# Loads and copies in pieces behind the value blocks of an attention kernel, its heads turned a block later

## The chip, the cores and the metric

One core of a Trainium2 chip runs the kernel. Its time is the device time of one execution in microseconds. TensorE (PE) multiplies matrices, VectorE (DVE), ScalarE (ACT) and GpSimd (POOL) do the rest, and SyncE (SP) issues every DMA, in one queue, in order. 16 DMA engines move the bytes.

## The reference

A token matrix of 2048 x 512 is layer-normalised. One branch is softmax attention with 32 heads of 16, the other a bilinear feed-forward of width 1792; the output is `x + attention * silu(feed-forward)`.

```python
xn = layernorm(x)
q, k, v = heads(xn @ wqkv)                    # 32 heads of 16
s = (softmax(q @ k.T * 16 ** -0.5) @ v) @ wo
g = silu(((xn @ w_gate) * (xn @ w_up)) @ w_down)
out = x + s * g
```

All is float32. Matmuls that need the precision run on rounded values (F32R) and their rests: `a = hi + lo`, three products in place of one.

## The kernel before, in words

**Units and tiles.** Attention goes by 32 units: a group of four heads (8 groups, `g`) times a quarter of the queries (`c`). Unit `i` is group `i // 4`, quarter `i % 4`. Each unit has 16 key tiles of 128; counted through, there are 512 tiles, `n`. For each tile and head one score matmul `t` (line 751) gives 128 keys x 512 queries, ScalarE takes its exponential into `e` (line 753), and `pv` (line 772; `last` in the last unit) multiplies `e` by the values. The maximum that the exponential needs is folded into the matmul as two more rows of `qs`. For that, all scores are computed a first time the other way round (`s`, line 729), 86 matmuls ahead of the `t`, and VectorE reduces each (`mx`, line 731). When a unit's maxima are complete, `maxima(i)` reduces and transposes them (`mm`, `mt`), stores them (`MD<-mt`) and loads them back as rows (`qs<-MD`).

**Cycles.** The main loop takes five tiles a cycle: 20 `t`, 20 `s` and a *filler*, a pair of sums with 24 to 30 matmuls in each half of the array's rows. Their order within a cycle is written out in `ORDERS`, or dealt evenly by `even` where the table has no entry. A cycle ends with `values`: the value matmuls of its five tiles, with other engines' steps placed before and behind them (`before_values`, `behind_values`). The filler, a generator, gives first the remaining projections (`p`, `proj_pair`), then the feed-forward (`g`, `u`, `y`), then the output product of the quarters that are done (`z`, `ending`). `Filler.begin` says at a cycle's start how many of the pair's matmuls the cycle takes. Where the generator yields nothing, because what the next pair needs isn't ready, the cycle has no filler.

**Order.** TensorE, ScalarE, VectorE and GpSimd run in program order. SP isn't in the list of ordered engines: up to tile 17 its DMAs are tied to program order (`Tied.on = n < 18`), later a scheduler orders them, and a DMA can be issued far ahead of its place in the program, once its buffers and data allow.

**What the change touches.**

- `proj_pair` copies two projections out of PSUM (`qr`); behind the value block `store` splits each into `hl` (one buffer) and `qk_store` writes it to DRAM (`KD<-hl`, `QD<-hl`).
- `load_k(g)` reads a group's keys from `KD` into one of two buffers `ks`. For groups 0 and 1 that is done by quarters of the keys, from group 2 on in two DMAs of 768 KB. It stands at the first tile of a group's second unit, for the group after. Scores of the next group begin 21 tiles ahead of it.
- The rounded inputs of quarters 1 to 3, `xh` and `xl`, are copied to DRAM (`XD`), six DMAs of 1 MB, each pair behind one of the projections of cycles 2 to 4, not before that projection's copy (`BEHIND`). The feed-forward reads them back later.
- `finish(i)` turns a unit's summed values: transpose `tr` (line 799), reciprocal, product on GpSimd, transpose back (line 810), store `OD<-acc`. It is a generator that `values` advances, once before and once behind the block. When it ends, the unit is `finished`, and `prepare` may load its heads for the output product.
- In the last cycles: 501 to 505 has the pair `z2_0`, 506 to 509 has `z2_2`, 510 and 511 have none.

Of the kernel before, what the change touches and what calls it, by code (L numbers as in the profile page):

```python
# [31 lines left out]
LEAD = 86  # L32
PAIRS = 4 * (NG // 2 - 1) + 1 + NC * (NF + 6)
BLOCK = 5
SOON = 8
ORDERS = {
# [30 lines left out]
}  # L67
SHORT = {65: 3, 68: 3}
HALF = (65, 491)
EBUFS = 20  # L70
HBUFS = 1
QBUFS = 2
# [12 lines left out]
def body(ctx, tc, x, wqkv, wo, wg, wu, wd, out):  # L85
# [512 lines left out]
    def ending():  # L598

        fp = fst["fp"]  # L600
        hi, lo = [fp.tile([P, 5, 512], F32R, name=n) for n in ("hl", "dh")]
        kept, added = [fp.tile([P, 5, 512], F32, name=n) for n in ("hh", "dl")]
        ops[0] = [(hi[:, d], lo[:, d]) for d in range(ND)]
        wrh, wrl = hi[:, 4], lo[:, 4]
        side = keep.tile([P, 2, 4, 512], F32, name="ks0")
        turn = [0]

        def until(c):
            while len([v for v in split_done if v[0] == c]) < ND:
                yield  # L610

        def rows_of(c, t):
            return x[(4 * c + t) * P:(4 * c + t + 2) * P].rearrange("(t p) d -> p t d", p=P)

        def two_tiles(c, t):
            yield from until(c)
            here = side[:, turn[0] % 2]
            turn[0] += 1
            got = [(here[:, n], here[:, 2 + n]) for n in range(2)]

            def loads():
                dma(here[:, 0:2], YD[c][:, t:t + 2])
                dma(here[:, 2:4], rows_of(c, t))
            soon(2, loads)
            two = Pair([("misc", f"z{c}_{u}") for u in (t, t + 1)], [o_terms(c, u) for u in (t, t + 1)])
            yield two
            for n, o in enumerate(two.outs):
                before_values.append(lambda u=t + n, o=o, got=got[n]: end(c, u, o, *got))

        rest = {}  # L630

        def begin_pair(t):
            yield from until(NC - 1)
            sums, more = [[tile[:, t + n] for n in range(2)] for tile in (kept, added)]
            rest.update({t + n: (sums[n], more[n]) for n in range(2)})
            for n in range(2):
                tt = 4 * (NC - 1) + t + n
                soon(2, lambda n=n, tt=tt: dma(more[n], x[tt * P:(tt + 1) * P]))
            ts = [o_terms(NC - 1, u) for u in (t, t + 1)]
            two = Pair([("misc", f"z{NC - 1}_{u}") for u in (t, t + 1)], [a[:-3] for a in ts], [a[-3:] for a in ts])  # L640
            yield two
            outs = two.outs
            nc.scalar.activation(sums[0], outs[0], AF.Copy)
            before_values.append(lambda: nc.vector.tensor_copy(sums[1], outs[1]))

        def gate_pair(t):
            for u in (t, t + 1):
                sums, more = rest[u]
                pool.tensor_tensor(sums, sums, fst["y"][:, u], op=OP.mult)
                pool.tensor_tensor(sums, sums, more, op=OP.add)  # L650

        yield from begin_pair(0)
        yield from begin_pair(2)
        ops[1] = small_tiles()
        wr = fp.tile([P, D], F32, name="wdr", bufs=2)
        pool.memset(wr, 0.0)
        for j in range(4):
            dma(wr[32 * j:32 * j + DH], wo[(H - 4 + j) * DH:(H - 3 + j) * DH])
        yield from two_tiles(0, 0)
        yield from two_tiles(0, 2)  # L660
        ops[2] = ops[0]
        behind_values.append(lambda: gate_pair(0))
        yield from two_tiles(1, 0)
        behind_values.append(lambda: gate_pair(2))

        def last_rows():
            pool.tensor_copy(wrh, wr)
            pool.tensor_tensor(wrl, wr, wrh, op=OP.subtract)
            for j in range(0, P, 32):
                dmar(wrh[j + DH:j + 32], wrh[j:j + DH])  # L670
        behind_values.append(last_rows)
        yield from two_tiles(1, 2)
        yield from two_tiles(2, 0)
        yield from two_tiles(2, 2)
        while "t" not in fst:
            yield
        banks = []
        for t in range(4):
            banks.append(psum("b", f"z{NC - 1}_{t}"))
            for n, r in enumerate((wrh, wrl)):  # L680
                nc.tensor.matmul(banks[t], fst["t"][:, t * P:(t + 1) * P], r, start=n == 0, stop=n == 1)
        Tied.on, sync.last, pool.last = True, None, None
        for t in range(4):
            end(NC - 1, t, banks[t], fst["y"][:, t], rest[t][0])
# [16 lines left out]
    def load_k(g, cs=range(NC)):  # L701
        heads = slice(64 * (g % 2), 64 * (g % 2) + 64)
        for e in range(2):
            k = ks[g % 2][64 * e:64 * e + KB]
            if g < 2:
                for c in cs:
                    dmar(k[:, :, c * 512:(c + 1) * 512], two(KD[0][c][heads], e))
            else:
                dmar(k, two(KD[g // 2][heads], e))

    def other_keys(_):
        ks.append(keep.tile([P, 2, S], F32R, name="ks1"))
# [48 lines left out]
    def part_block(i, todo):  # L761

        g = i // NC
        whole = i == NU - 1
        if whole and todo[0][1] == 0:
            fst["last"] = psum("s", "last")
        o = fst["last"] if whole else psum("b", f"pv{i}")
        for n, (_, kt, es) in enumerate(todo):
            halves = [slice(0, 256), slice(256, 512)] if whole and kt == NT - 1 else [slice(0, 512)]
# [20 lines left out]
    def finish(i):  # L790

        g, c = divmod(i, NC)
        tr = keep.tile([P, 16, 32], F32, name="tr", bufs=1)
        acc = sums.pop(i)
        late = i >= NU - NC
        flat = "p b e -> p (b e)"
        if not late:
            yield
        nc.vector.transpose(tr.rearrange(flat), acc)
        rc = keep.tile([P, 16, 1], F32, name="rc", bufs=1)  # L800
        if NU - NC <= i < NU - 2:
            yield
        nc.vector.reciprocal(rc, tr[:, :, DH:DH + 1])  # L803
        over = rc.to_broadcast([P, 16, DH])
        (nc.vector if i >= NU - NC else pool).tensor_tensor(tr[:, :, 0:DH], tr[:, :, 0:DH], over, op=OP.mult)
        if not late:
            yield
        elif i < NU - 2:
            yield
        nc.vector.transpose(acc, tr.rearrange(flat))  # L810
        dma(OD[c][4 * g:4 * g + 4], acc)
        finished.add(i)
# [150 lines left out]
    def filler(wq0):  # L963
        yield from proj_pair(0, [(wq0, 0, 2), (wq0, 0, 3)])
        for m in range(1, NG // 2):
            wk, wq = fst["qk", m]
            for c in range(NC):
                if c == 2 and m + 1 < NG // 2:
                    fst["qk", m + 1] = qk_weights(m + 1, 1), qk_weights(m + 1, 0)
                yield from proj_pair(m, [(wk, 1, c), (wq, 0, c)])  # L970
                if m == 1 and c:
                    after = fst["high"].ins.name
                    for n, src in enumerate((xh, xl)):
                        put = sync.dma_start(XD[c][n].bitcast(F32), src[c].bitcast(F32))
                        tc.add_manual_dep(put.ins, after, BEHIND, reason="not before the first exponentials")
                if m == NG // 2 - 1 and c == NC - 2:
                    nxt = gu_weights(0)
        run_all(before_values)
        run_all(behind_values)
        flush()  # L980
        qkv.close()
        fst["fp"] = ffp.enter_context(tc.tile_pool(name="ffn", bufs=1, reuse_waits="tile"))
        yield from ffn(nxt)

    finished = set()
    now = [0]
    heads, last_group = [], []

# [4 lines left out]
    class Filler:  # L993
# [6 lines left out]
            if self.pair is self:  # L1000
                self.pair, self.done = None, True

        def begin(self, whole):

            if not self.pair and not self.done:
                self.fetch()
            if not self.pair:
                return [0, 0]
            left = self.pair.left()
            return left if whole or left[0] <= self.pair.first[0] else list(self.pair.first)  # L1010

        def item(self, h):
            self.pair.emit(h)
# [3 lines left out]

    def values(rounds):
        run_all(before_values)
        step_small(heads)  # L1020
        run_all(reduced)
        if gates:
            gates.pop(0)()
        block(rounds)
        run_all(behind_values)
        step_small(heads)

    ready, reduced, gates = {}, [], []

# [3 lines left out]
    def place(h):  # L1033
# [6 lines left out]
        if n not in ready:  # L1040
# [2 lines left out]
            if kt == 6 and i + 2 < NU:  # L1043
                load_q(i + 2)
            if kt == 0 and g + 1 < NG and c == 1:
                load_k(g + 1)
            ready[n] = i, kt, [None] * 4
        es = ready[n][2]
        es[j] = expo(i, kt, j)
# [31 lines left out]
    with tc.manual_schedule(engines=ORDERED):  # L1081
# [4 lines left out]
        while n < NU * NT:  # L1086
            tiles = min(SHORT.get(n, BLOCK), NU * NT - 2 - n) or 2
            ends = n + tiles == NU * NT
            if m == TOTAL and place_of:
                place_of.close()  # L1090
                place_of = ctx.enter_context(banks_of(LATE_BUFS)) and None
            if fil.done:
                fil = Filler(ending())
            f = fil.begin(n not in HALF)
            last = min(4 * (n + tiles), TOTAL - 4 * (not ends))
            nt, ns = last - q, min(last + LEAD, TOTAL) - m
            q, m = q + nt, m + ns
# [21 lines left out]
        while fil.pair or not fil.done:  # L1119
# [2 lines left out]
            if not fil.pair:  # L1122
                fil.fetch()
            while fil.pair:
                for h, left in enumerate(fil.pair.left()):
                    if left:
                        fil.item(h)
                        break
            flush()
    ffp.close()  # L1130

# [15 lines left out]
```

## Time and profile before

| | |
|---|---|
| median of 3 runs | 1699.65 us (1699.35 to 1699.77) |
| the profiled execution | 1698.56 us |
| its span | 1696.8 us |
| TensorE busy, mean granted clock | 98% of the span, 0.992 |
| VectorE, ScalarE, GpSimd busy | 84%, 70%, 43% |
| DMA | 145.93 MB, 86 GB/s over the span |
| key loads | 16 of 192 KB, 12 of 768 KB |
| stores of `hl` | 30 of 512 KB and 30 of 256 KB |

The profile was taken in one execution, whose time stands 1.1 us under the median. TensorE's busy time says that it was at work, not that it ran at its peak. Rows of a chain give start, duration, engine, line; rows of waits give total, times, longest; rows of SP give start and the time that issuing took, and say nothing of when the bytes landed.

### The profile page before, as it was taken

What the parts mean: (1) busy time and instruction counts of PE and PEld (TensorE: products, weight loads), DVE (VectorE), ACT (ScalarE), POOL (GpSimd) and SP (SyncE); (2) the same over time, 40 slices, a digit from 0 to 9 for tenths busy, and PEclk for the clock granted to TensorE, in tenths of its full rate; (3) what the DMA queues carried; (4) which work ended last, traced back from release to release, by engine and by line L of the source; (5) the groups of instructions that cost most, each with busy time, mean ns of one, the idle gap of its engine ahead of it and who ended that gap; (6) DMA issues with size and microseconds to landing.
All of it is one profiled execution on the core that took longest, in us unless ns stands there. A gap on an engine that the chain in (4) does not pass through costs nothing.

```text
span 1696.8 us, 35187 instructions
## 1 busy us (share of the span) xinstructions
PE 1664.9 (98%) x13702; PEld 1125.1 (66%) x13702; DVE 1422.0 (84%) x2477; ACT 1189.3 (70%) x2553; POOL 736.6 (43%) x772
## 2 busy tenths in 40 slices
PE   9999899799999999999999999999999999999997
PEld 6776577466766666667666766676667666766654
DVE  7888698688888998889889888898889888888942
ACT  6367577576776777677677876776778676777775
POOL 5213343552542637346252653534347254446361
PEclk9999899899999999999999999999999999999999
DMA  6217533521222322412025221331325121133231
GB/s 232 89 48 210 214 135 113 146 73 30 66 68 58 95 70 80 79 54 62 23 71 128 80 61 36 81 58 52 104 61 118 30 66 46 47 99 104 71 116 69
DMA packets 117843, 145.93 MB, mean 86 GB/s; under 512 B 12781, under 2 KB 74477, under 8 KB 114989
## 3 DMA queue, kind: packets, MB, share of 16 engines
q1 hardware_dynamic: 117676, 143.69, 29.3%
q8 instruction: 108, 1.77, 0.4%
q14 instruction: 59, 0.48, 0.1%
HBM read 95.94 MB, written 47.45 MB: 85 GB/s over the span
## 4 chain that ended last, share of the span: by engine, by line
PE 89%; DVE 5%; DMA 2%; issue 1%; POOL 1%; ACT 0%; SPq 0%; DVEq 0%; POOLq 0%; ACTq 0%
PE pv L772 24%; PE s L729 15%; PE t L751 13%; PE u L354 10%; PE g L354 9%; PE y L354 8%; DVE mx L731 4%; PE p L354 4%; PE z L354 2%; DMA KD<-hl 1%; PE last L772 1%; PE v L306 1%; PE v L326 1%; PE v L330 1%; PE p L306 1%
## 5 line engine op out<-in xcount | busy, mean ns | idle before, releaser
L731 DVE TENSOR_REDUCE mx<-s 128x1 f32<-128x512 f32 x2048 | 1245.1, 684 | 170.4 <-PE t L751 127.6
L753 ACT ACTIVATE e<-t 128x512 f32<-128x512 f32 x2048 | 1025.4, 659 | 34.0 <-PE t L751 27.8
L751 PE MATMUL t<-qs,ks 50*128 50x512 f32 x2048 | 789.5, 406 | 3.3 <-DVE mx L731 0.9
L729 PE MATMUL s<-ks,qs 48*128 48x512 f32 x2048 | 757.8, 407 | 9.2 <-ACT part L785 5.3
L729 PEld LDWEIGHTS s<-ks,qs 48*128 48x128 f32 x2048 | 369.5, 186 | 145.4 <-issue 79.0
L772 PE MATMUL pv<-e,V 128*32 128x512 f32 x3968 | 446.5, 595 | 0.0
L751 PEld LDWEIGHTS t<-qs,ks 50*128 50x128 f32 x2048 | 374.8, 186 | 68.9 <-ACT e L753 16.5
L99 POOL TENSOR_TENSOR acc<-acc,part 128x512 f32<-128x512 f32 x93 | 120.5, 1295 | 445.4 <-ACT part L785 445.4
L772 PEld LDWEIGHTS pv<-e,V 128*32 128x32 f32 x3968 | 118.7, 110 | 265.0 <-issue 256.0
L785 ACT ACTIVATE part<-pv 128x512 f32<-128x512 f32 x93 | 55.7, 598 | 327.4 <-PE pv L772 314.9
L354 PE MATMUL g<-fh,w1h 64*128 64x512 f32 x448 | 180.9, 404 | 0.0
L354 PE MATMUL u<-fh,w0h 64*128 64x512 f32 x448 | 177.3, 396 | 0.0
L354 PE MATMUL g<-fh,w1l 64*128 64x512 f32 x448 | 177.1, 395 | 0.0
L354 PE MATMUL g<-fl,w1h 64*128 64x512 f32 x448 | 177.0, 395 | 0.0
L354 PE MATMUL u<-fl,w0h 64*128 64x512 f32 x448 | 176.5, 394 | 0.0
L354 PE MATMUL u<-fh,w0l 64*128 64x512 f32 x448 | 175.5, 392 | 0.0
L354 PE MATMUL y<-dh,hl 64*128 64x512 f32 x448 | 146.9, 393 | 0.0
L354 PE MATMUL y<-dh,hh 64*128 64x512 f32 x448 | 144.6, 395 | 0.0
L354 PE MATMUL y<-dl,hh 64*128 64x512 f32 x448 | 143.6, 394 | 0.0
L99 POOL TENSOR_TENSOR tr<-tr,rc 128x256 f32<-128x256 f32 x28 | 17.4, 622 | 220.6 <-DVE rc L803 220.6
L354 PEld LDWEIGHTS g<-fh,w1l 64*128 64x128 f32 x448 | 83.8, 187 | 5.5
L354 PEld LDWEIGHTS g<-fh,w1h 64*128 64x128 f32 x448 | 83.3, 186 | 4.3
(228 smaller groups left out, 2341.6 us busy)
## 6 DMA issues: line engine op xcount, KB each, us to landing
w1r<-in_wg_dram SPq DMA_DIRECT2D x56, 256.0 KB
w0r<-in_wu_dram SPq DMA_DIRECT2D x56, 256.0 KB
wdr<-in_wd_dram SPq DMA_DIRECT2D x56, 256.0 KB
qs<-QD SPq DMA_DIRECT2D x64, 192.0 KB
ks<-KD SPq DMA_DIRECT2D x12, 768.0 KB
KD<-hl SPq DMA_DIRECT2D x16, 512.0 KB
OD<-acc SPq DMA_DIRECT2D x31, 256.0 KB
QD<-hl SPq DMA_DIRECT2D x14, 512.0 KB
```

What stands on the lines that cost most here:

```text
L99: got = getattr(self.engine, name)(*args, **kw)
L306: nc.tensor.matmul(o[:, part], l(d), r(d)[:, part], start=k == d == 0 and not begun, stop=k == 2 and d == ND - 1, skip_group_check=begun)
L326: nc.tensor.matmul(outs[k], l[LOWER], r[LOWER], start=k == 0 and n == 0, stop=(stop or k == 0) and n == len(low) - 1, skip_group_check=k == 1)
L330: nc.tensor.matmul(outs[1 - k], l[UPPER], r[UPPER], start=k == 0 and m == 0, stop=(stop or k == 0) and m == len(high) - 1, skip_group_chec ...
L354: nc.tensor.matmul(self.outs[k], l[rows], r[rows], start=opens and not half, stop=closes, skip_group_check=half == 1)
L729: nc.tensor.matmul(o, QS[i][b:b + KB, pr, t * P:(t + 1) * P], k[b:b + KB, pr, kc * 512:(kc + 1) * 512], start=True, stop=True)
L731: nc.vector.tensor_reduce(MX[i][:, j, t, kc:kc + 1], o, axis=AX.X, op=OP.max)
L751: nc.tensor.matmul(o, k[b:b + KR, pr, kt * P:(kt + 1) * P], QS[i][b:b + KR, pr], start=True, stop=True)
L753: nc.scalar.activation(e, o, AF.Exp, scale=DH ** -0.5)
L772: nc.tensor.matmul(o[32 * j:32 * j + 32, c], V[:, kt, h0:h0 + 32], es[j][:, c], start=(kt if whole else n) == 0, stop=kt == NT - 1 if whol ...
L785: nc.scalar.activation(part, o, AF.Copy)
```

## The change

Key loads from group 2 on are cut into quarters like those before; all go through a list, `bulk`, at whose front they are put, and of which `values` runs up to four entries behind a block. The copies of the inputs are cut into pieces of 256 KB, go through the same list, and lose their dependency on the projection's copy. `values` advances the heads once, not twice, runs complete maxima ahead of them, and `finish` loses its first pause. `SOON`, from 8 to 12, lets maxima run in the middle of a cycle that ends up to two tiles ahead of a unit. The table `LIMIT` takes the place of `HALF`; the bank `last` is taken earlier; the last loop takes the longer half first and runs the waiting steps.

```diff
-SOON = 8
+SOON = 12
...
-HALF = (65, 491)
+LIMIT = {65: 12, 491: 12}
+BULK = 4
...
         yield from two_tiles(2, 2)
+        yield
         while "t" not in fst:
...
-                dmar(k, two(KD[g // 2][heads], e))
+                for c in cs:
+                    part = slice(c * 512, (c + 1) * 512)
+                    dmar(k[:, :, part], two(KD[g // 2][heads][:, :, part], e))
...
-        if whole and todo[0][1] == 0:
-            fst["last"] = psum("s", "last")
...
         flat = "p b e -> p (b e)"
-        if not late:
-            yield
         nc.vector.transpose(tr.rearrange(flat), acc)
...
-                    after = fst["high"].ins.name
-                    for n, src in enumerate((xh, xl)):
-                        put = sync.dma_start(XD[c][n].bitcast(F32), src[c].bitcast(F32))
-                        tc.add_manual_dep(put.ins, after, BEHIND, reason="not before the first exponentials")
+                    bulk.extend(lambda n=n, src=src[c], c=c, d=d: dma(XD[c][n][:, d].bitcast(F32), src[:, d].bitcast(F32))
+                                for n, src in enumerate((xh, xl)) for d in range(ND))
...
         run_all(behind_values)
+        run_all(bulk)
         flush()
...
-            if not self.pair:
-                return [0, 0]
-            left = self.pair.left()
-            return left if whole or left[0] <= self.pair.first[0] else list(self.pair.first)
+            return [min(limit, n) for n in self.pair.left()] if self.pair else [0, 0]
...
         run_all(before_values)
+        run_all(reduced)
         step_small(heads)
-        run_all(reduced)
         if gates:
             gates.pop(0)()
         block(rounds)
         run_all(behind_values)
-        step_small(heads)
+        for _ in range(BULK):
+            if bulk:
+                bulk.pop(0)()
...
-                load_k(g + 1)
+                bulk[:0] = [lambda g=g, c=c: load_k(g + 1, [c]) for c in range(NC)]
...
+                fst["last"] = psum("s", "last")
...
-                for h, left in enumerate(fil.pair.left()):
-                    if left:
-                        fil.item(h)
-                        break
+                left = fil.pair.left()
+                fil.item(left.index(max(left)))
+            run_all(before_values)
+            run_all(behind_values)
             flush()
```

More of the change, by code (lines that the diff above doesn't have):

```diff
@@ L983, in filler @@
         yield from ffn(nxt)
-    finished = set()
+    bulk, finished = [], set()
     now = [0]
@@ L1001, in fetch, with begin @@
                 self.pair, self.done = None, True
-        def begin(self, whole):
+        def begin(self, limit):
             if not self.pair and not self.done:
                 self.fetch()
-            if not self.pair:
-                return [0, 0]
-            left = self.pair.left()
-            return left if whole or left[0] <= self.pair.first[0] else list(self.pair.first)
+            return [min(limit, n) for n in self.pair.left()] if self.pair else [0, 0]
         def item(self, h):
@@ L1091, in body @@
                 place_of = ctx.enter_context(banks_of(LATE_BUFS)) and None
+                fst["last"] = psum("s", "last")
             if fil.done:
                 fil = Filler(ending())
-            f = fil.begin(n not in HALF)
+            f = fil.begin(LIMIT.get(n, 99))
             last = min(4 * (n + tiles), TOTAL - 4 * (not ends))
```

## The prediction

> **What bounds the kernel now.** I read the page's engine shares first, then the windows by stage, the chain of waits, and last the queue of the DMA issues.
>
> ```profile
> PE 1664.9 (98%) x13702; PEld 1125.1 (66%) x13702; DVE 1422.0 (84%) x2477; ACT 1189.3 (70%) x2553; POOL 736.6 (43%) x772
> ```
> ```profile
> 165.00:180.00 15.00, 7.58 (x58) 3.17 (x54) 4.53 (x9) 2.77 (x5) 2.89 (x4) 0.82 0.91 316
> ...
> 300.00:325.00 25.00, 15.92 (x117) 9.32 (x111) 11.85 (x21) 10.39 (x23) 11.13 (x13) 0.79 0.87 203
> ...
> 345.00:610.00 265.00, 265.00 (x2250) 180.42 (x2244) 230.79 (x400) 189.74 (x411) 114.76 (x120) 1.00 0.25 65
> ```
>
> The columns after the window are its length, then busy time of PE, PEld, DVE, ACT, POOL, granted clock, DMA share and GB/s. From 345 to 610 us TensorE never idles: nothing done to queues can help there, and the change takes no matmul away. The two windows with holes are the exception: TensorE works 7.58 of 15 us and 15.92 of 25 us, and the granted clock falls too. In both the DMA share is about 0.9. The chain of waits says what the holes are:
>
> ```profile
> 135.04 4.43 PE pv L772 x40
> ...
> 163.63 11.54 DMA KD<-hl
> ...
> 191.87 4.43 PE pv L772 x40
> ...
> 267.40 4.43 PE pv L772 x40
> 282.43 4.43 PE pv L772 x40
> 297.46 3.62 PE pv L772 x32
> 302.66 11.02 DMA KD<-hl
> ...
> 315.74 1.26 POOL acc L99
> ...
> 329.45 2.74 PE pv L772 x24
> ```
> ```profile
> POOL hl L99 <- DMA KD<-hl: 55.2, 9, 13.8
> ```
>
> `hl` has one buffer, so POOL can't split the next projection before the store of the last one has landed. A store takes 11 us here, because others are in the queue:
>
> ```profile
> 139.94 0.34 SPq L99 DMA_DIRECT2D XD<-xh  x1
> ...
> 155.40 4.25 SPq L99 DMA_DIRECT2D ks<-KD  x8
> ...
> 162.34 1.62 SPq L99 DMA_DIRECT2D KD<-hl  x2
> ...
> 300.69 0.46 SPq L99 DMA_DIRECT2D ks<-KD  x1
> ...
> 302.18 0.86 SPq L99 DMA_DIRECT2D KD<-hl  x2
> 303.09 0.53 SPq L99 DMA_DIRECT2D ks<-KD  x1
> ```
>
> Hole 1: three value blocks (pv) later the clock should read 135.04 + 3 x 15.03 (282.43 to 297.46 is one ordinary cycle), or 180.1; it reads 191.87. Price 11.7 us. Hole 2: the first short cycle runs from the end of one value block to the next undisturbed, the second doesn't:
>
> ```profile
> 308.01 2.78 PE L772 MATMUL pv<-e,V 128*32 128x512 f32 x24
> ```
>
> From 301.9 (297.46 plus 4.43) to 308.01 is 6.1 us; the second short cycle has the same work and would reach its block at 310.8 + 6.1 = 316.9, but reaches it at 329.45. Price 12.6 us. Together 24.3 us, 1.4% of the run, re-warming of the clock included.
>
> **The change part by part.** *Copies of the rounded inputs.* Six DMAs of 1 MB become 24 of 256 KB, at most four behind a value block. In hole 1 copies (from 139.94 on) and the 1.5 MB key load (155.40) lie in the queue ahead of the store at 162.34. By program order they are now dealt over seven blocks: 1 MB, then the key load alone, then 1 MB per block. A block's stores are 1.5 MB, so no 15 us holds over about 3.5 MB with the weights; the 316 GB/s of the window above would carry 4.7 MB. But the tie to the exponentials is gone as well, and SP's order is free from tile 18 on. The last fence shows what that means: the key load written at tile 80 is issued at 300.69, near tile 65, as soon as its buffer is free. So the 20 copies written after tile 18, and the second group's key load, may rise into the opening, where their inputs lie ready. Either way the stores of hole 1 are rid of them. I take 11.0 us of the 11.7.
>
> *In the opening* 5 MB of copies and 1.5 MB of keys would then meet the first group's loads:
>
> ```profile
> 52.54 0.79 SPq L99 DMA_DIRECT2D ks<-KD  x2
> ```
> ```profile
> 58.19 0.87 PE L729 MATMUL s<-ks,qs 48*128 48x512 f32 x4
> ```
>
> The third quarter of the keys is loaded at 52.54, and by the order of scores first used at 58.19. At the 316 GB/s of hole 1 each megabyte ahead of that load costs 3.3 us; one lies inside the slack, two don't, and the fourth quarter can be met again. Ends 0 and +7; I take +1, since the copies become ready one by one and most before 40 us.
>
> *Key loads.* Two issues of 768 KB become eight of 192 KB for each of groups 2 to 7. Each quarter of `ks` is last read at tiles 3, 7, 11 and 15 of the unit before. If a quarter is released by itself, as the two halves already are (300.69 and 303.09), 384 KB is issued every four tiles and only the last quarter meets the store at 302.18: 0.4 MB in place of 1.5 MB. At the 203 GB/s of that window 1.15 MB less are 5.7 us; the POOL addition at 315.74 then comes at 310.0, and the value block behind it, whose sum needs its buffer, ends at 310.8. I take 11.5 us of the 12.6. If it isn't released by itself the gain may be 0. In groups 3 to 7 no store of `hl` from a projection runs, and nothing waits: 0.
>
> *Heads one block later.* Both transposes stood at one boundary:
>
> ```profile
> DVE acc L810 <- POOL tr L99: 19.8, 27, 0.7
> ```
> ```profile
> 269.89 0.71 DVE L799 STREAM_TRANSPOSE tr<-acc 128x512 f32<-128x512 f32 x1
> ```
>
> VectorE waits 0.73 us for POOL in each of 27 units. The cycle that begins at 267.40 holds such a turn and takes 15.03 us like the next, which has none: it is covered by the 4.43 us of pv. Where other VectorE work falls at the same boundary it may show; of the 19.8 us I take -1, ends -3 and 0. The store of the heads leaves 15 us later; its buffer is needed three blocks on, so that is free, but for the end (below).
>
> *Maxima mid-cycle.* Twelve in place of eight catches the cycles that end two tiles ahead of a unit; counting through the loop, six of them. Both kinds already exist:
>
> ```profile
> 436.13 4.43 PE pv L772 x40
> 451.66 4.43 PE pv L772 x40
> ...
> 744.58 4.44 PE pv L772 x40
> 759.93 4.43 PE pv L772 x40
> ```
> ```profile
> 447.02 0.21 DVE L740 STREAM_TRANSPOSE mt<-mm 128x32 f32<-128x32 f32 x1
> ...
> 747.65 0.21 DVE L740 STREAM_TRANSPOSE mt<-mm 128x32 f32<-128x32 f32 x1
> ```
>
> With maxima mid-cycle (447.02) the cycle takes 15.53; with maxima at the boundary (747.65), two tiles ahead of the unit, 15.35. So this edit gains nothing: 6 x 0.18, +1 us, ends -2 and +2.
>
> *The end.* This is the part that costs. Unit 30's heads are finished in the second step of the block at tiles 491 to 495; that step is gone, so they are finished at the next block's start, after the loop has asked for the next output pair. That pair needs those heads. Following the loop's counts, the cycle of tiles 501 to 505 gets no pair, its pair goes to 506 to 509, and the last pair to the last two tiles, which had none.
>
> ```profile
> 1650.66 4.43 PE last L772 x40
> ...
> 1663.78 4.43 PE last L772 x40
> ...
> 1676.00 3.57 PE last L772 x32
> ...
> 1682.15 3.02 PE last L772 x24
> ```
> ```profile
> 1642.66 9.91 ACT L753 ACTIVATE e<-t 128x512 f32<-128x512 f32 x20 [3.05 <-PE t L751]
> ```
> ```profile
> 1676.90 1.28 DVE L589 TENSOR_TENSOR ks<-ks 128x512 f32<-128x512 f32 x2
> ```
>
> The emptied cycle hardly shortens (13.12 from 1650.66 to 1663.78): 20 exponentials and the wait for pv are 12.96 of it, so -0.2. The last two tiles get 48 matmuls beside their 8: 28 pairs side by side, at the ordinary cycle's cadence of (15.03 - 4.43)/44 = 0.24 us, are 6.7 us, where now 2.6 lie between 1679.57 (1676.00 plus 3.57) and 1682.15: +4.1. Two additions of the last pair, 1.28 us, now stand on VectorE ahead of the last products: +1.0. Together +4.9, ends +2 (the last matmuls run under other waits) and +7. The limit at 491, the earlier bank for `last` and the last loop's order give the same counts as before: 0.
>
> **The sum**, against the profiled run's 1698.56: -11.0 -11.5 +1.0 -1.0 +1.0 +4.9 = -16.6, or 1682.0. The median of the runs is 1.1 above the profiled one: 1683.
>
> **Rivals.** *The second hole stays.* The load still rises to where its buffer is free, all eight pieces at 300 us if quarters aren't released singly. For it: both halves rose in this way (300.69 and 303.09). Against it: they rose apart, each as it was released. Time 1683 + 11.5 = 1694.5. *The opening pays.* Copies meet the loads of the first keys twice: 1683 + 6 = 1689. With both, 1700: no change that can be told. *The pieces hold the queue: slower.* SP issues in order; a piece put ahead of the maxima's rows waits for its quarter's last reader.
>
> ```profile
> SPq L99 <- PE t L751: 22.4, 5, 8.7
> ```
> ```profile
> 1241.24 1.96 DMA MD<-mt
> 1243.87 2.10 DMA qs<-MD
> ```
>
> Such waits reach 8.7 us now, and a row's trip is 4.1. If each of six group loads makes the next unit's rows late by one trip, that is 24 us: 1707; it decides from 2.8 us a load. Against it: today's waits of this kind delay no matmul in 345 to 610. The Trainium skill, "DMA: Bandwidth & Descriptors", the section on measured bandwidth, tells to batch transfers to 1 MiB; from its 0.95 us for 64 KB and 6.15 us for 1 MB I estimate 4.8 us for 768 KB and 6.6 for four quarters. By that rule twelve halves would cost 21.6 us more transfer, and 1705 if all were exposed; the windows' DMA share of 0.25 speaks against any exposure. *It doesn't do what it says*: SP's order stays such that both holes stay, and only the end's cost is left: 1704.
>
> **How the numbers follow.** Forecast 0.60, second hole stays 0.12, opening pays 0.11, both 0.05, pieces hold the queue 0.07, both holes stay 0.05. About 0.2% (3.4 us) can be told from no change here. Faster: 0.60 + 0.12 + 0.11 = 0.83; same 0.05; slower 0.12. The forecast's own range is 1677 (both holes gone whole, end +2) to 1688; with the two milder rivals 1677 to 1695, which leaves out 0.17.
>
> **What would show it.** Right: no stretch before 350 us with a granted clock under 0.9; the value blocks of hole 1 45 to 46 us apart in threes; the wait of POOL on the key store far under 55.2 us; `ks` pieces before 300 us; copies of the inputs in the opening or one megabyte a block. At the end, no z matmuls between the first two blocks `last`, and 6 to 7 us ahead of the last one. Wrong: a hole that stays, scores in the opening that wait for `ks`, or the queue waiting on t ahead of the maxima's rows.

## The result, and the profile after

The changed kernel takes 1687.01 us, median of 4 runs (1685.45 to 1689.85); beside it the kernel before took 1699.71 (1699.35 to 1699.96). The ratio is 0.9927, 95% interval 0.991 to 0.9945: 0.73% faster, inside the predicted range and 4 us above the predicted time. The profiled execution took 1685.45 us with a span of 1683.7, 13.1 less than before, and the sections below account for that span.

The windows of the changed kernel over the two stretches that had the holes (columns as before):

```profile
165.00:180.00 15.00, 15.00 (x127) 9.63 (x126) 13.47 (x27) 10.94 (x25) 5.69 (x6) 1.00 0.19 71
300.00:325.00 25.00, 23.11 (x182) 15.86 (x182) 22.06 (x37) 18.32 (x38) 17.81 (x19) 0.93 0.39 126
```

The first window is full at full clock, with a DMA share of 0.19 where 0.91 stood. The second still loses 1.9 us, at a clock of 0.93; in its parts from 300 to 305 and from 305 to 310 us the clock is 0.88 and 0.78. So one sign that the prediction named, no stretch before 350 us under 0.9, did not come. The chain of waits gives the holes' lengths and the end:

```profile
134.88 4.43 PE pv L774 x40
...
180.87 4.43 PE pv L774 x40
...
286.02 3.61 PE pv L774 x32
291.79 6.58 DMA KD<-hl
...
300.45 1.28 POOL acc L100
301.75 0.72 DVE tr L799
...
309.38 2.77 PE pv L774 x24
...
1629.95 4.43 PE last L774 x40
1643.20 7.14 PE last L774 x39
1658.17 3.57 PE last L774 x32
1669.21 1.90 PE last L774 x24
```

Three cycles of hole 1 now take 45.99 us (134.88 to 180.87), where before had 56.83. Hole 2, from the block at 286.02 to the one at 309.38, takes 23.36 where 31.99 stood; a store still stands in it, and it lands in 6.58 us, not 11.02. The end, from the first block `last` to the end of the span, takes 1683.7 - 1629.95 = 53.75, where before had 46.14.

The queue of the DMA issues says where the loads and copies went (start, issuing time):

```profile
27.30 1.80 SPq L100 DMA_DIRECT2D XD<-xl  x4
...
150.50 2.69 SPq L100 DMA_DIRECT2D XD<-xh  x4
...
253.54 1.14 SPq L100 DMA_DIRECT2D ks<-KD  x2
...
289.34 0.46 SPq L100 DMA_DIRECT2D ks<-KD  x1
...
290.80 0.42 SPq L100 DMA_DIRECT2D ks<-KD  x1
291.31 0.85 SPq L100 DMA_DIRECT2D KD<-hl  x2
```

Copies of the inputs are issued from 27.30 on, and in hole 1 only the four at 150.50 are left. The keys of group 2 are loaded a quarter at a time from 253.54, as each is released, and only the last quarter (289.34 and 290.80) lies ahead of the store at 291.31. GpSimd's wait on the key store fell from 55.2 us in total, 13.8 at the longest, to the row below. That is the way that was forecast, though not "far under 55.2":

```profile
POOL hl L100 <- DMA KD<-hl: 37.2, 9, 7.7
```

Term by term, profile against profile:

| term | predicted | measured |
|---|---|---|
| hole 1 | -11.0 | 45.99 - 56.83 = -10.8 |
| hole 2 | -11.5 | 23.36 - 31.99 = -8.6 |
| opening (first block of the chain above, 135.04 before) | +1.0 | -0.2 |
| the rest (heads -1, maxima +1) | 0 | -1.1 |
| end | +4.9 | 53.75 - 46.14 = +7.6 |
| sum | -16.6 | -13.1 |

### The profile page after: what moved, and what is told of

The parts are those of the page before. It is cut to its first block, busy times and chain, and to the rows that moved or that the text cites. A ratio compares the mean times of both kernels' runs of the same rounds, so it can differ in the third digit from the quotient of the medians.

```text
span 1683.7 us, 35313 instructions
## 1 busy us (share of the span) xinstructions
PE 1667.0 (99%) x13702; PEld 1123.8 (67%) x13702; DVE 1418.4 (84%) x2477; ACT 1188.1 (71%) x2553; POOL 736.6 (44%) x772
## 4 chain that ended last, share of the span: by engine, by line
PE 96%; DVE 2%; ACT 0%; DMA 0%; POOL 0%; issue 0%; SPq 0%; DVEq 0%; POOLq 0%; ACTq 0%
PE pv L774 26%; PE s L733 16%; PE t L755 14%; PE g L355 10%; PE u L355 9%; PE y L355 9%; PE p L355 4%; PE z L355 2%; DVE mx L735 2%; PE last L774 1%; PE v L307 1%; PE v L327 1%; PE p L307 1%; PE warm L865 0%; DMA KD<-hl 0%; PE xT L283 0%
```

## The experiments

The theory to be tested: hole 1 goes because copies and keys are no longer ahead of its stores; hole 2 shrinks because the keys come by quarters; the end pays because unit 30's heads are finished a block too late for the loop. Rivals: the heads' edit, not the quarters, shortens hole 2; one of hole 1's two edits does all; the end's price lies in the last two tiles' matmuls and not in the missing pair. The kernels ran on other chips than the first comparison, where the kernel before had medians of 1700.5 to 1701.9, so ratios and the stages' lengths are compared, not times. The end runs from the first block `last` to the end of the span.

| kernel | ratio to before, 95% | span | hole 1 | hole 2 | end |
|---|---|---|---|---|---|
| before | | 1696.8 | 56.83 | 31.99 | 46.14 |
| changed | 0.9927 (0.991 to 0.9945) | 1683.7 | 45.99 | 23.36 | 53.75 |
| end_step_back | 0.988 (0.9866 to 0.9894) | 1675.7 | 45.97 | 23.55 | 46.24 |
| warm_501 | 1.0023 (1.0013 to 1.0032) | 1698.0 | 45.7 | 22.81 | 69.3 |
| keys2_held | 0.9895 (0.9882 to 0.9909) | 1682.9 | 45.92 | 19.58 | 55.11 |
| keys_whole | 0.9928 (0.9913 to 0.9943) | 1684.5 | 45.55 | 26.42 | 52.07 |
| before_keys | 0.9995 (0.9973 to 1.0017) | 1700.8 | 57.8 | 29.44 | 48.93 |
| before_heads | 1.0003 (0.9994 to 1.0012) | 1700.9 | 56.3 | 28.74 | 54.67 |
| heads_before | 0.9908 (0.9893 to 0.9922) | 1684.4 | 45.75 | 29.88 | 47.59 |
| copies_held | 0.9917 (0.9903 to 0.993) | 1683.9 | 45.75 | 25.66 | 52.37 |
| copies_before | 0.9927 (0.9911 to 0.9944) | 1689.0 | 48.13 | 23.08 | 54.95 |
| keys1_in_place | 0.9922 (0.9907 to 0.9937) | 1683.9 | 49.50 | 21.55 | 52.12 |
| best | 0.9858 (0.9839 to 0.9877) | 1672.6 | 45.61 | 19.50 | 46.28 |
| best_soon8 | 0.9847 (0.9833 to 0.9862) | 1673.3 | 45.26 | 19.51 | 46.17 |

Each length comes from one profile. In hole 2 the changed kernel, end_step_back and warm_501, which differ only at the end, lie at 22.81 to 23.55; versions that differ from it only in the copies or in group 1's keys lie at 21.55 to 25.66. So a difference of 2 or 3 us in hole 2 is a direction, not a size.

**The end: end_step_back.** The changed kernel, with the heads' second step back behind the block at tiles 491 to 495 only:

```diff
         for _ in range(BULK):
             ...
+        if rounds[-1][0] == NU - 2:
+            step_small(heads)
```

> The changed kernel, but behind the value block of tiles 491 to 495 the heads' step is run as before, so that the last two output pairs stand in cycles 501 and 506 again. Theory A (the end costs 7.6 us because these heads come one block late, 4.9 of it the moved pair and 2.7 a halved clock in the emptied cycle): from the first value block of the last unit to the span's end 46.1 us in place of 53.8, granted clock 1.00 there, profiled run near 1678, and the runs spread less than the 4.4 us of the changed kernel. Rival B (the end got longer through the store of heads or the queue): 53 us stay, 1685.

The chain of waits of this kernel, at the end:

```profile
1629.46 4.43 PE last L774 x40
...
1654.78 3.57 PE last L774 x32
...
1660.94 3.02 PE last L774 x24
```

The end is 1675.7 - 1629.46 = 46.24, that of before, and the last two tiles take 6.16 (1654.78 to 1660.94) where the changed kernel had 11.04. So in this pair of profiles the whole +7.6 comes from this one missing step. The size isn't fixed: in the changed kernel and the five versions of it that keep its end without added matmuls, the end takes 52.07 to 55.11 us. The last two tiles take 11.03 to 11.05 in each of them; what varies most is the value blocks before and behind the emptied cycle, which take from 4.43 to 7.14 us. That the runs of end_step_back would lie closer together was wrong: they spread over 5.3 us (1678.13 to 1683.46).

**The clock in the emptied cycle: warm_501.** The windows of the changed kernel there show more than missing matmuls:

```profile
1635.00:1640.00 5.00, 4.72 (x13) 1.99 (x10) 0.00 (x0) 5.00 (x11) 1.17 (x2) 0.84 0.67 191
1640.00:1643.00 3.00, 3.00 (x7) 1.66 (x6) 0.00 (x0) 3.00 (x7) 0.71 (x1) 0.50 0.00 0
1643.00:1647.00 4.00, 4.00 (x21) 0.99 (x24) 0.00 (x0) 1.80 (x4) 0.00 (x0) 0.50 0.00 0
```

With only `t` to do, at ScalarE's pace, the granted clock falls to 0.50 by 1640, and the value block that follows takes 7.14 us in place of 4.43. Yet TensorE is idle for only 0.28 us of these 12. The Trainium skill, "TensorE: Matmul & The Clock Gate", Part 1, puts the throttle down to an idle window of about 3.4 us. Here no gap between TensorE's rows comes near that; whether what the page calls idle is what the profile counts as idle isn't shown. The experiment adds matmuls whose results nobody reads, one ahead of each `t` of this cycle:

```diff
+                if n == 501:
+                    wh = fst["w"][0]
+                    nc.tensor.matmul(psum("misc", "warm"), wh[:, 0, 0:P], wh[:, 1], start=True, stop=True)
```

> The changed kernel with 20 matmuls of 128x128x512 on weights that are at hand, one ahead of each t of the emptied cycle 501 to 505; nobody reads their sums. Theory A (the clock is halved because the t alone, one each half microsecond, keep TensorE too idle): the clock stays at 1.00 through this cycle, the next cycle (14.97 us in the changed kernel) takes 12.2 to 12.4, the profiled run is 2.5 us faster, near 1683, although TensorE does more. Rival B (the cycle got longer because of the pair's own waits): the next cycle stays at 15, and the time at 1685 or above.

It went the other way, and not by rival B's cause either, since the next cycle took 13.7 us and not 15: 1704.91 us, and the cycle's two value blocks are 30.12 us apart (1628.72 and 1658.84). TensorE's rows of this kernel, then its windows:

```profile
1635.66 0.50 PE L1103 MATMUL warm<-fh 128*128 128x512 f32 x1
1636.09 0.50 PE L755 MATMUL t<-qs,ks 50*128 50x512 f32 x1
...
1639.24 0.79 PE L755 MATMUL t<-qs,ks 50*128 50x512 f32 x1
1639.96 0.79 PE L1103 MATMUL warm<-fh 128*128 128x512 f32 x1
```
```profile
1640.00:1650.00 10.00, 10.00 (x15) 3.97 (x14) 0.00 (x0) 4.18 (x7) 0.00 (x0) 0.50 0.00 0
```

The matmuls follow one another 0.43 us apart and then, at half clock, 0.72, where those of an ordinary cycle are 0.24 apart. The engine counts as busy all 10 us and the clock stays at 0.50. A matmul's row includes the load of its weights, though: the last one shown and its weight load both start at 1639.96, and the window counts 3.97 us of weight loads (its second figure). So a TensorE that the profile counts as busy without a gap doesn't hold the clock by that alone; how full the array must be for it, these runs don't tell. Theory A's forecast failed; whether idleness isn't the cause, or these matmuls don't count against it, the run can't tell. What is shown is that the cycle with its ordinary pair keeps its clock: in end_step_back it is 1.00 from 1629.46 to 1642.57.

**Hole 2: keys2_held, keys_whole, before_keys.** The first holds the loads of group 2 behind the exponentials, so that they can't rise among the stores. The second is the changed kernel with its key loads in two halves again. The third is the kernel before with the halves cut into quarters and nothing else.

```diff
# keys2_held
...
+                    if g == 2:
+                        tc.add_manual_dep(put.ins, fst["exp"].ins.name, BEHIND, ...)
# keys_whole
-                for c in cs:
-                    part = slice(c * 512, (c + 1) * 512)
-                    dmar(k[:, :, part], two(KD[g // 2][heads][:, :, part], e))
+                if 0 in cs:
+                    dmar(k, two(KD[g // 2][heads], e))
# before_keys, against the kernel before
-                dmar(k, two(KD[g // 2][heads], e))
+                for c in cs:
+                    part = slice(c * 512, (c + 1) * 512)
+                    dmar(k[:, :, part], two(KD[g // 2][heads][:, :, part], e))
```

> The changed kernel, with the key pieces of group 2 alone kept behind an exponential near tile 80, so that none of them is in the queue with the last projections' stores. Theory A (what is left of the second hole, 4 us, is the last quarter of the keys ahead of a store): the store lands 1 to 2 us sooner, the stretch between the value blocks at 286 and 309 us takes 20 to 21 us in place of 23.4, clock 1.00, time 3 us less, 1682 for the profiled run. Rival B (what is left is the weights, the queries' load and the one buffer hl): 23 us stay, 1685.

> The changed kernel, with the key loads of groups 2 to 7 in two DMAs of 768 KB again. Theory A (quartering closes most of the second hole, since each quarter is released by itself): the hole comes back by 8 to 9 us, the two value blocks around it are 32 us apart, time 1695. Rival B (it was closed by the heads' later turn or by the copies being gone): 23.4 us stay, 1686.

> The kernel before with quartered key loads alone, for groups 2 to 7. Theory A (the two holes are independent): the second hole shrinks from 12.6 to about 4 us, the first stays, 1691. Rival B (they come from one cause, a full queue, and quarters alone don't help): 1699.

The chain of keys2_held, then of keys_whole, then of before_keys:

```profile
286.01 4.43 PE pv L776 x40
...
296.58 2.77 PE pv L776 x24
...
305.59 2.71 PE pv L776 x24
```
```profile
286.13 3.62 PE pv L773 x32
...
291.34 9.90 DMA KD<-hl
...
312.55 2.78 PE pv L773 x24
```
```profile
298.37 4.47 PE pv L774 x40
...
304.62 7.55 DMA KD<-hl
...
314.24 1.25 POOL acc L99
...
318.03 1.26 POOL w0l L99
319.29 0.59 POOL tr L99
319.90 0.71 DVE acc L812
...
327.81 2.32 PE pv L774 x17
```

Without the loads hole 2 is gone: 305.59 - 286.01 = 19.58, no store in the chain. The span is only 0.8 us shorter than the changed kernel's, since the end of this profile, where the clock was lost in more cycles, takes 1.4 more and the cycles between 1.6. With halves the store lands in 9.90 us, and the hole is 3.1 longer than the changed kernel's: not the 8 to 9 us of theory A, and the ratio, 0.9928, is that of the changed kernel. In the kernel before the quarters cut the store from 11.02 to 7.55, yet the hole only by 2.6 (31.99 to 29.44). The rows say why: behind the addition, which ends at 315.49, GpSimd splits two weight tiles (the last step of that is `w0l`) and comes only at 319.29, 3.8 us later, to the heads' product `tr`, and VectorE's second transpose waits for that at 319.90, with the next maxima behind it. The store's 3.5 us are gained, but from the addition on the chain is no shorter. This version as a whole is no faster (0.9973 to 1.0017), as rival B had it, but not by its cause: its profile is 1.6 us ahead of before's when hole 2 ends, and loses that and 4 us more by the end of the span, most of it after 1637 us. There the cycle of tiles 501 to 505 took 14.24 us instead of 13.12, after a granted clock of 0.84 from 1648 to 1652 us.

**The heads: before_heads, heads_before.** The first is the kernel before with the heads' edit alone, the second the changed kernel without it, but for the `yield` on the first line below, a pause in the opening, which stays.

```diff
# before_heads, against the kernel before; heads_before is the reverse, against the changed one, but for the first line
+        yield
...
-        if not late:
-            yield
...
+        run_all(reduced)
         step_small(heads)
-        run_all(reduced)
...
-        step_small(heads)
```

> The kernel before with the heads' edits alone: first pause gone, one step a block, maxima ahead of them. Theory A (this edit is no gain in the cycles and costs at the end): slower by 6 to 8 us, about 1706, with the last unit's 53 to 54 us in place of 46. Rival B (turning the heads later shortens the cycles): 1698 or less.

> The changed kernel with the heads turned as before: both pauses, two steps a block, maxima behind the first. Theory A (in the second hole VectorE's second transpose waited for POOL behind the weights, 3 us; at the end the old place saves 7.5; in other cycles nothing): the stretch with the two short cycles takes 26 to 27 us in place of 23.4, the end 46 in place of 53.8, so 4 us faster, 1681 to 1682. Rival B (the heads' turn is worth nothing in the hole): 23.4 us stay there, 1678.

The chain of heads_before:

```profile
285.71 4.43 PE pv L774 x40
...
301.42 1.28 POOL acc L100
...
306.51 0.59 POOL tr L100
307.12 0.71 DVE acc L812
...
315.59 2.71 PE pv L774 x24
```

The same chain as in before_keys, and a hole of 29.88. In the changed kernel the addition, at nearly the same time (300.45), is followed by VectorE's `tr` at once (301.75). So the heads' edit is worth 6.5 us in hole 2 beside the quarters, where about 3 were expected, and 3.3 alone (28.74), because there the store, 11.09 us of landing, is late again. Quarters alone give 2.6, both 8.6. The rival that the heads' edit shortens hole 2 is thus the larger part of the truth. At the end the edit costs: before_heads has 54.67 where before has 46.14, and as a whole it gains nothing (1.0003); 6 to 8 us slower was expected.

**Hole 1: copies_held, copies_before, keys1_in_place.** The first keeps the pieces, but each again not before the projection's copy. The second puts the six copies of 1 MB back. The third loads the second group's keys in place again.

```diff
# copies_held
...
+    def held(dst, src):
+        put = sync.dma_start(dst, src)
+        tc.add_manual_dep(put.ins, fst["high"].ins.name, BEHIND, ...)
# copies_before
-                    bulk.extend(...)
+                    after = fst["high"].ins.name
+                    for n, src in enumerate((xh, xl)):
+                        put = sync.dma_start(XD[c][n].bitcast(F32), src[c].bitcast(F32))
+                        tc.add_manual_dep(put.ins, after, BEHIND, ...)
# keys1_in_place
-                bulk[:0] = [lambda g=g, c=c: load_k(g + 1, [c]) for c in range(NC)]
+                if g == 0:
+                    load_k(1)
+                else:
+                    bulk[:0] = [lambda g=g, c=c: load_k(g + 1, [c]) for c in range(NC)]
```

> The changed kernel, with each piece of the input copies made to wait for the projection copied last when it is dealt, so that none rises into the opening and they go out a megabyte behind each block up to tile 45. Theory A (it is enough that they don't stand with the first group's key load and the stores in one cycle; whether they rise or are dealt is the same): first hole stays closed, three cycles from 135 us take 46 us, time 1685 within 1. Rival B (rising into the opening is what closes the hole): POOL's waits on the stores grow and 3 to 8 us come back, 1689 to 1693.

> The changed kernel, with the input copies as before: six DMAs of 1 MB, each behind its projection's copy. The key load of group 1 still rises into the opening. Theory A1 (the copies and the key load together made the first hole): half of it or more stays closed, 0 to 5 us come back, 1686 to 1690. Rival A2 (the copies alone made it): 10 us come back, 1696.

> The changed kernel, with the key load of group 1 issued where it stood before, in eight DMAs at the first tile of unit 1, in order; the input copies stay in pieces. With copies_before it splits the first hole (10.8 us closed). Theory A (the key load just ahead of a store is most of it, as 2 us came back with the old copies): 3 to 8 us come back, the three cycles from 135 us take 49 to 54 us, 1689 to 1693. Rival B (it takes both together): 46 us stay, 1685.

The chain of copies_before, then of keys1_in_place:

```profile
135.12 4.50 PE pv L774 x40
...
183.25 4.43 PE pv L774 x40
```
```profile
135.25 4.43 PE pv L774 x40
...
154.37 4.96 DMA ks<-KD
159.35 10.10 DMA KD<-hl
...
184.75 4.43 PE pv L774 x40
```

Of a hole of 11 us, copies back leave 2 (48.13), the key load back leaves 3.5 (49.50); with both back, as in the kernel before, it is 56.83. So either edit closes most of it; that a block's stores still fit beside one of the two loads is the reading that agrees with this, and no run measures it apart. That the copies rise into the opening isn't needed: with copies_held they are dealt by fours behind the blocks, and the hole is as short (45.75).

**The best of both: best, best_soon8.** end_step_back and keys2_held together; the second has `SOON = 8` as well.

> The changed kernel with both repairs: the heads' step back at the block of tiles 491 to 495, and the key pieces of group 2 kept behind an exponential near tile 80. Theory A (the two losses are separate, 7.5 us at the end and 3.8 us in the second hole): profiled run near 1675, the last unit's 46 us, the stretch with the two short cycles 19.6 us, some 11 us faster than the changed kernel. Rival B (the output pairs of the end lose the clock in other cycles instead): 1678 to 1682, no better than the step alone.

> The same with the maxima's bound at 8 as before. Theory A (moving maxima of six units to mid-cycle trades one half microsecond for another): the same time within 1 us; the cycles of tiles 25 to 29 and 30 to 34 take 15.0 and 15.5 in place of 15.5 and 15.0. Rival B (mid-cycle maxima spare a wait for the rows): 2 to 3 us slower.

Both are the fastest here: 1676.21 us (0.9858) and 1675.44 (0.9847). The two gains add up: 1683.7 - 7.5 for the end - 3.8 for hole 2 is 1672.4, and best has a span of 1672.6. In best the cycle of tiles 501 to 505, with its pair, has the full clock of 1.00.

The edit of `SOON` can't be told from nothing: the intervals overlap, and the spans differ by 0.7 us, in the other direction than the medians. The exchange that was expected is there: the two cycles from 165.44 us take 15.03 and 15.30 in best_soon8, those from 165.47 take 15.53 and 15.02 in best.

## Why the prediction was right, and where it was off

**The bound and hole 1: right.** Full queues delay the stores that GpSimd waits for; -10.8 against -11.0. The argument priced copies and keys together and did not say what either is worth: taking away only one of them leaves 2 to 3.5 us. The rise into the opening happened as said, but it isn't what closes the hole.

**The opening: right that it costs little.** 0.2 us less, where +1 was taken. The rival "the opening pays" fell: copies were issued from 27.30 on and the first blocks came no later.

**Hole 2: the step that failed is "I take 11.5 us of the 12.6", for the quarters alone.** Quarters were released singly, as argued, and the store landed 4.4 us sooner. But the step followed the chain only to the addition, and took the rest of the hole to go with it. Behind it stood GpSimd's splits, `tr` and VectorE's transpose, which before_keys shows as the next bound: 2.6 us for the quarters. The profile before has this already, behind the addition of 315.74, in its chain and in VectorE's rows:

```profile
317.63 1.29 POOL w1l L99
318.93 2.48 DMA w1r<-in_wg_dram
321.42 0.71 DVE acc L810
```
```profile
321.41 0.71 DVE L810 STREAM_TRANSPOSE acc<-tr 128x512 f32<-128x512 f32 x1 [3.38 <-DMA w1r<-in_wg_dram]
```

VectorE waits 3.38 us here. The wait is put down to a DMA, so it isn't among the 19.8 us that the prediction read for `acc<-tr`; GpSimd's product `tr`, which the transpose reads, starts only at 320.76, behind four operations that split two weight tiles. The heads' edit, which the prediction counted as covered by pv with -1 for the whole kernel, takes those off the chain and is worth 3.3 to 6.5 us here. It was costed in an ordinary cycle. In the changed kernel the store lands 4.4 us sooner, and from its landing to the value block at 309.38 it is 11.0 us, where before had 15.8. And one quarter still rises ahead of the store; those last 3.8 us go only when the loads are held (keys2_held). So 8.6 of 12.6, by two edits.

That the total still came within 4 us is in part luck: an edit that was priced at next to nothing made up for most of what the quarters fell short. With hole 2 as long as in heads_before, 6.5 us more, an estimate from these profiles puts the changed kernel at 1693.5, outside the predicted range.

**Heads and maxima elsewhere: right in size.** The rest of the kernel gained 1.1 us, against 0. That maxima mid-cycle gain nothing agrees with best_soon8, which shows no difference that can be told.

**The end: right in kind, +7.6 in place of +4.9.** The pairs moved as counted, and end_step_back gives the whole price back. The last two tiles cost +4.9 (6.15 to 11.04) where the step took +4.1. The +1.0 for VectorE's additions did not come: from the last value block to the end of the span it is 14.5 us, before 14.7. The emptied cycle itself hardly changed (13.25 against 13.12), near the -0.2 that was taken. What the sum left out is the cycle behind it: 14.97 us (1643.20 to 1658.17) against 12.22, +2.75, of which the value block alone, 7.14 in place of 4.43 us, at half clock for its first 4 us, is 2.7. The step "the emptied cycle hardly shortens ... so -0.2" counted the work rightly and didn't price the clock that the emptied cycle hands on. That the thin filling is what lowers the clock is the reading that agrees with end_step_back; warm_501 didn't confirm it.

**The rivals on the queue fell.** No key load held up the maxima's rows by an amount that shows: the rest of the kernel is no longer than before. (A row's trip, put at 4.1 us, is 4.7 from 1241.24 to the end of the load; the 4.1 leave out the gap between store and load.) The Trainium skill, "DMA: Bandwidth & Descriptors", section "Bandwidth", tells to batch transfers to 1 MiB or more; the prediction's estimate from its table, which holds transfers that GpSimd issued, was up to 21.6 us for the quarters. These runs show no such cost: before_keys, with quarters alone, is at 0.9995, and its store behind them landed sooner.

**What stays open.** The runs of the changed kernel spread over 4.4 us, those of before on that chip over 0.6. The chip's clock takes part (0.991 to 0.995 in the four runs, the longer spans with the lower clock), but end_step_back, without the emptied cycle, spreads as far, and on another chip the kernel before does too (1698.47 to 1703.62 in 15 runs). One of the ten runs of before_keys took 1715.51 us at a granted clock of 0.943. In several profiles, one of them of before_keys, a cycle of tiles 491 to 505 lost the clock, so the cause isn't the emptied cycle alone.

## What to carry to other kernels

When a wait is taken away, follow the chain past it through every engine to the next matmul, since the second thing that was late there decides the gain; here two edits that gave 2.6 and 3.3 us alone, each in one profile, gave 8.6 together. A wait that the profile puts down to a DMA can hide the engine that stands behind it. Where a scheduler may issue a load as soon as its buffer is free, a load that isn't urgent needs a dependency that keeps it from the stores that are. And before moving a step later, look at the last units: a step that is free in every steady cycle can empty one at the end and cost both its work and the clock.

## What the hardware showed unexpectedly

The granted clock fell to 0.50 with TensorE idle for 0.28 of 12 us, when it had only single `t` matmuls at ScalarE's pace, and stayed there for some 20 us in warm_501 although the rows of its matmuls, each with its weight load, followed one another without a gap: 0.43 us apart, then 0.72. That cost 2.7 us in the changed kernel; in warm_501, with 20 added matmuls, the cycle took 30.12 us in place of 13.25. A stage in which the profile says that TensorE is busy can therefore still lose its clock, and only the granted clock shows it.

Four loads of 192 KB in place of each of 768 KB cost nothing that could be measured (0.9995, interval 0.9973 to 1.0017), and a key store behind them landed in 7.55 us where it took 11.02.
